# Prefix sums from a softplus in two parts, gates and loads further ahead, tokens turned before the scores, another join with the first MLP

## The chip, the cores and the metric

One core of one Trainium2 chip runs the whole program. The metric is the device time of one execution in microseconds (us). Five engines work at the same time, each through its own list of instructions in order: PE (matmuls and transposes, with weight loads that overlap them), DVE, ACT, POOL, and SP, which issues the DMAs here. Semaphores order them.

## What is computed

A gated linear attention over 4 batches, 8 heads, 768 tokens and a head size of 48, then two MLPs over the 384 channels:

```python
f = 1.0 / (1.0 + np.exp(-f_logit))
for t in range(S):
    state = f[:, :, t, :, None] * state + np.einsum('bhd,bhe->bhde', k[:, :, t], v[:, :, t])
    y[:, :, t] = np.einsum('bhd,bhde->bhe', q[:, :, t], state)
...
u = x + (xt @ U @ V)                    # tokens mixed, rank 32
x = u + np.maximum(u @ w_ch1, 0.0) @ w_ch2
h = np.maximum(x @ w_in, 0.0)           # second MLP, with a convolution of 3 taps
out = (h * sigmoid(conv(h))) @ w_out
```

Everything is float32. The second weights are float64 in memory and are put together from their two words on the chip.

## The kernel before

The attention works in 24 chunks of 128 tokens (6 for each batch), one pass of the loop `for i in range(1, NG)` for each, and chunk 0 ahead of it. For a chunk, `gate_max` and `gates` make sp = ln(1 + exp(-f)) (DVE or POOL, then two steps on ACT); `prefix` sums it along the tokens with one matmul with the triangular matrix `tri` (tile n), and ACT makes exp(-n) and exp(n) of it (a, b); `hats` multiplies q and k with these (qh, kh, from chunk 6 on POOL); `turn` transposes qh and kh (qTp, kTp) and ACT copies the result (qT, kT); `scores` multiplies them (s), `mask` applies the triangle on DVE (p, two instructions), `out_chunk` makes y from p and v and from qT and the state w, and adds to the state (kv); `state_end` brings the state on (wtmp on DVE, w on POOL), and `out_evac` copies y into u32 on ACT (u). Then `tokens` transposes a finished chunk's u (xt), ACT rounds it (xh), DVE makes the rest (xl), `mix_in` multiplies both with U (z), and after the sixth chunk of a batch `mix_z` (zu, zt, zz, zst) and six `mix_out` (mix, added into u on DVE) follow in the next three passes.

A value in two parts, such as xh and xl, is rounded to the type fp32r, and the remainder stands beside it; products of fp32r are made in one matmul each. `prefix` multiplies plain float32.

The order of the work on every engine is that of the code. In a pass i of the middle of the loop, f is loaded for chunk i + 4, k and q for i + 3, v for i + 2; `gate_max` and `gates` work on chunk i + 3, `prefix` and `hats` on i + 2, scores and output on i, `turn` on i + 1. All PSUM banks are named by hand: xt and the first `mix_out` of a pass share bank 0, n has bank 6. sp has two buffers, f, k and q three, v four.

DVE also prepares the first weights of the MLPs between this (cvt, cvg, `slot`, so many steps a pass as `slots(i)` says); the last step of such a piece runs at the head of the next pass (ACT cast, POOL difference w1l or w2l). One of them, cwp, transposes the taps on PE in bank 0.

After the last chunk, `mlps` runs the first MLP in units of 128 hidden columns (a, rh, rl, b), on halves of 512 tokens; `split1` makes uh and ul for a half. What is left of the attention is put between its matmuls by `hooks`.

Of the kernel before, what the change touches and what calls it, by code (L numbers as in the profile page):

```python
# [9 lines left out]
F32 = mybir.dt.float32  # L10
# [25 lines left out]
def kernel(  # L36
# [168 lines left out]
    def mlps(ms, banks, pieces, late, checks, hooks):  # L205
# [44 lines left out]
        def split1(t, i, engines):  # L250
            for kk in range(KD):
                split(u32[:, kk, t * T1 + i * HT:t * T1 + (i + 1) * HT], uh[:, kk, halves1[i]], ul[:, kk, halves1[i]], engines[i])

        def up1(u, i):
            t, j = divmod(u, J1)
            ps = bank(i, [128, HT], f"a{i}")
            up(w1hv, w1lv, j, halves1[i], (uh, ul), ps, lambda kk: hooks.pop((u, i, kk), int)())
            if (u, i) == (1, 0):
                down1(0, 0)
            rh = rg.tile([128, HT], F32R, tag="rh", name="rh")  # L260
            rl = rg.tile([128, HT], F32R, tag="rl", name="rl")
            nc.scalar.activation(out=rh, in_=ps, func=ACTF.Relu)  # L262
            nc.vector.scalar_tensor_tensor(  # L263
                out=rl, in0=ps, scalar=0.0, in1=rh.bitcast(F32), op0=ALU.max, op1=ALU.subtract)
            rt[1, u, i] = rh, rl
            hooks.pop((u, i, KD), int)()
            if j == J1 - 1:
                if t + 1 < NT:
                    split1(t + 1, i, (nc.vector, nc.gpsimd))
                else:  # L270
                    split_u(0, (i,))
# [157 lines left out]
        yield  # L429
        split1(0, 0, (nc.gpsimd, nc.vector))  # L430
        yield
        split1(0, 1, (nc.gpsimd, nc.vector))
        yield
# [58 lines left out]
        return banks.tile(shape, F32, tag=f"k{i}", name=name)  # L492

    tri = gc.tile([128, 128], F32, name="tri")
    ga = gc.tile([128, NG, NP], F32, name="ga")
    dr = gs.enter_context(tc.tile_pool(name="gdr", bufs=1, space=bass.MemoryType.DRAM))
    ends_d = dr.tile([NG, 1, NP * 128], F32, name="ends_d")
# [47 lines left out]
    def gates(g):  # L545
        sp = sps[g] = spt.pop(g)
        nc.scalar.activation(out=sp, in_=sp, func=ACTF.Exp, scale=-1.0)
        nc.scalar.activation(out=sp, in_=sp, func=ACTF.Ln, bias=one, scale=1.0)  # L548

    def prefix(g):  # L550
        n = bank(6, [128, DM], "n")
        mm(n, tri, sps.pop(g).rearrange("p h d -> p (h d)"), True, True)
        nv = n.rearrange("p (h d) -> p h d", h=H)
        b_ = ga1.tile([128, H, D], F32, tag="b", name="b")
        eng = nc.vector if g < DVE_HATS else nc.gpsimd
# [105 lines left out]
    def out_chunk(g):  # L661
        yt[g] = ps = bank(4, [128, KD, C], "y")
        qq, vv, pp = qT.pop(g), vt[g], pt.pop(g)
        started = set()

        def part(gr, lhsT, rhs):
            m, c = divmod(gr, 4)
            return c, ps[32 * c:32 * (c + 1), m, :], lhsT, rhs

        if g % NCH:  # L670
            w = w_t[g % 2]
            strips([part(3 * p + x, w[:, p, 32 * x:32 * (x + 1)], qq[:, p, :])
                    for p in range(NP) for x in range(3)], started)
        strips([part(3 * p + gr, vv[:, 128 * p + 32 * x:128 * p + 32 * (x + 1)], pp[j][:, p, :])
                for x, gr, j in ((0, 0, 0), (1, 1, 0), (2, 1, 1), (3, 2, 1)) for p in range(NP)], started)
        if (g + 1) % NCH:
            strips(state(g), set())
        vt.pop(g)

# [86 lines left out]
    with tc.manual_schedule():  # L766
# [5 lines left out]
        )  # L772
        nc.vector.memset(one, 1.0)
        nc.vector.memset(ga, 1.0)
        for t, x in ((a_t[0], 1.0), (q_t[0], 0.0), (k_t[0], 0.0)):
            nc.vector.memset(between(t), x)
        for t in w_t:
# [54 lines left out]
                    late_work.append(steps.pop(0))  # L832

        def slots(i):
            return (0, 6) if i == 1 else (0, 0) if i < 5 else (2, 2) if i < 8 else (1, 2)

        def mix_next():
            nonlocal mixed
# [26 lines left out]
        gates(3)  # L865
        ends(2)
        for i in range(1, NG):
            load_of(f"f{i + 4}")
            for x in "kq":
                load_of(f"{x}{i + 3}")  # L870
            load_of(f"v{i + 2}")
            if i < NG - 1:
                ends_back(i + 1)
            if i > 1 and i % NCH:
                state_end(i - 1)
            if EARLY_GATES <= i < NG - 3:
                gate_max(i + 3)
            follow = slot_end()
            n_mix = 2 if mixq else 0
            if i == FILL_FROM + 1:  # L880
# [1 line left out]
            hats = prefix(i + 2) if 1 < i < NG - 2 else None  # L882
            if i != CATCH_UP + 1:
                mix_next()
            scores(i)
            if i == CATCH_UP + 1:
                mix_next()
            if hats and i >= EARLY_GATES:
                hats()
            if zq:  # L890
# [5 lines left out]
            if zq:  # L896
                zq.pop()()
            if i < EARLY_GATES:
                gate_max(i + 3)
            if hats and i < EARLY_GATES:  # L900
                hats()
            lows = []
            if i > 1:
                lows.append(tokens(turned))
                turned += 1
            if i + 1 < NG:
                turn(i + 1, "qT")
            if zs:
# [2 lines left out]
                step()  # L911
            if zq:
                zq[0] = zq[0]()
            if i < NG - 3:
                gates(i + 3)
            if i < FILL_FROM:
                slot(slots(i)[1])
            if i == 1:
# [35 lines left out]
        tokens(NG - 1, 6)()  # L954
        next(mlp)
        last = {}

        def last_z():
# [6 lines left out]
            last["z"] = last["z"]()  # L965

        def last_casts():
            last["z"]()()

        def last_ends():  # L970
# [178 lines left out]
```

## Time and profile before

| What | Value |
| --- | --- |
| median of 3 runs | 654.68 us (654.08 to 655.6) |
| the profiled execution, its own time | 654.5 us |
| its span, first to last instruction | 652.8 us |
| PE busy | 641.3 us, 98% |
| DVE busy | 424.9 us, 65% |
| ACT busy | 275.2 us, 42% |
| POOL busy | 145.6 us, 22% |

Attention takes the first 149 us of the span, the first MLP goes on to about 441 us, the second fills the rest. A busy share says only that an instruction was under way; matmuls overlap, so what a step costs on PE is read from the chain of waits, where each piece stands with the time by which it moved the chain on. A row of the timeline gives start, duration, engine, line, operation, output and inputs, and in brackets how long the engine had been idle before and for whom it waited.

### The profile page before, as it was taken

The page shows a single profiled execution, that of the slowest core. Times are in us where ns is not written, and L with a number is a line of the kernel's source. Part 1 is how long each engine was busy: PE and PEld are TensorE (multiplying, and loading weights), DVE is VectorE, ACT ScalarE, POOL GpSimd, SP SyncE. Part 2 cuts the span into 40 slices and gives each one's busy share as a digit, 9 for nine tenths or more (in the row PEclk, how much of TensorE's full clock was granted, in tenths as well). Part 3 has the DMA queues.
Part 4 walks back from the last instruction along what each step waited for, and adds up shares of the span by engine and source line. Part 5 has one row for each costly group of instructions (what it writes and reads, how often), then busy time and mean ns, then how long its engine had stood idle before and what let it go on. Part 6 is the DMA issues. An engine that isn't in the chain of part 4 may idle for free.

```text
span 652.8 us, 12695 instructions
## 1 busy us (share of the span) xinstructions
PE 641.3 (98%) x5146; PEld 559.3 (86%) x5146; DVE 424.9 (65%) x663; ACT 275.2 (42%) x524; POOL 145.6 (22%) x181
## 2 busy tenths in 40 slices
PE   8999999999999999999999999999999999999995
PEld 6788778777888788888888888889999999999995
DVE  4868876566666665666665334226988777787762
ACT  5779677853223232222232111123544644634533
POOL 1176678441222222111112000001120110110000
PEclk9999999999999999999999999999999999999999
DMA  9988898810333330222220466100000200200202
GB/s 181 171 163 168 168 175 155 148 51 2 96 98 96 98 97 1 73 73 73 72 73 0 126 193 190 48 0 2 1 0 1 73 2 0 74 2 1 72 1 78
DMA packets 132661, 50.56 MB, mean 77 GB/s; under 512 B 112900, under 2 KB 128285, under 8 KB 132595
## 3 DMA queue, kind: packets, MB, share of 16 engines
q1 hardware_dynamic: 132594, 49.67, 31.2%
q8 instruction: 42, 0.69, 0.4%
q14 instruction: 25, 0.20, 0.1%
HBM read 44.89 MB, written 4.76 MB: 76 GB/s over the span
## 4 chain that ended last, share of the span: by engine, by line
PE 94%; DVE 2%; ACT 1%; issue 1%; DMA 0%; POOL 0%; POOLq 0%
PE a L76 38%; PE b L76 38%; PE y L76 5%; PE s L76 4%; PE n L76 2%; PE kTp L598 2%; PE xt L688 1%; PE qTp L598 1%; PE z L76 1%; PE mix L76 1%; PE kv L76 1%; DVE p L619 1%; DMA f<-in_f_logit_dram 0%; ACT sp L548 0%; PE row L76 0%
## 5 line engine op out<-in xcount | busy, mean ns | idle before, releaser
L262 ACT ACTIVATE rh<-a 128x512 fp32r<-128x512 f32 x72 | 43.1, 599 | 221.9 <-PE a L76 217.6
L263 DVE SCALAR_TENSOR_TENSOR rl<-a,rh 128x512 fp32r<-128x512 f32 x72 | 49.8, 692 | 109.1 <-ACT rh L262 109.0
L76 PE MATMUL a<-uh,w1l 128*128 128x512 f32 x216 | 84.4, 391 | 0.0
L76 PE MATMUL a<-uh,w1h 128*128 128x512 f32 x216 | 84.2, 390 | 0.0
L76 PE MATMUL a<-ul,w1h 128*128 128x512 f32 x216 | 84.1, 389 | 0.0
L76 PE MATMUL b<-rh,w2l 128*128 128x512 f32 x216 | 84.1, 389 | 0.0
L76 PE MATMUL b<-rh,w2h 128*128 128x512 f32 x216 | 84.0, 389 | 0.0
L76 PE MATMUL b<-rl,w2h 128*128 128x512 f32 x216 | 84.0, 389 | 0.0
L76 PE MATMUL b<-woh,w1h 128*128 128x384 f32 x264 | 70.4, 335 | 0.0
L318 ACT ACTIVATE c<-c 128x768 f32<-128x768 f32 x31 | 26.3, 847 | 62.4 <-DVE c L348 62.4
L76 PEld LDWEIGHTS a<-uh,w1l 128*128 128x128 f32 x216 | 40.5, 188 | 10.0 <-POOL w1l L79 1.8
L76 PE MATMUL a<-w2h,winh 128*128 128x384 f32 x192 | 49.0, 336 | 0.0
L76 PEld LDWEIGHTS b<-woh,w1h 128*128 128x128 f32 x264 | 48.0, 188 | 0.0
L76 PEld LDWEIGHTS b<-rh,w2h 128*128 128x128 f32 x216 | 40.6, 188 | 8.5
L76 PEld LDWEIGHTS b<-rh,w2l 128*128 128x128 f32 x216 | 40.5, 188 | 8.5
L76 PEld LDWEIGHTS b<-rl,w2h 128*128 128x128 f32 x216 | 40.5, 188 | 8.4
L76 PEld LDWEIGHTS a<-ul,w1h 128*128 128x128 f32 x216 | 40.6, 188 | 8.3
L76 PEld LDWEIGHTS a<-uh,w1h 128*128 128x128 f32 x216 | 40.6, 188 | 8.1
L79 POOL TENSOR_TENSOR ul<-u,uh 128x512 fp32r<-128x512 f32 (+1 forms) x15 | 19.1, 1295 | 127.0 <-ACT uh L105 127.0
L76 PE MATMUL b<-wol,w1h 128*128 128x384 f32 x132 | 44.3, 335 | 0.0
L304 ACT ACTIVATE h<-a 128x384 f32<-128x384 f32 x64 | 30.9, 496 | 29.3 <-PE a L76 26.0
L619 DVE TENSOR_TENSOR p<-s,tri 128x512 f32<-128x512 f32 x48 | 30.9, 686 | 17.9 <-PE s L76 17.6
(138 smaller groups left out, 1336.3 us busy)
## 6 DMA issues: line engine op xcount, KB each, us to landing
raw<-in_moe_w_ch_dram SPq DMA_DIRECT2D x48, 384.0 KB
f<-in_f_logit_dram SPq DMA_DIRECT2D x24, 192.0 KB
k<-in_k_dram SPq DMA_DIRECT2D x24, 192.0 KB
q<-in_q_dram SPq DMA_DIRECT2D x24, 192.0 KB
v<-in_v_dram SPq DMA_DIRECT2D x48, 96.0 KB
raw<-in_moe_w_in_dram SPq DMA_DIRECT2D x8, 384.0 KB
raw<-in_moe_w_out_dram SPq DMA_DIRECT2D x8, 384.0 KB
out_dram<-o SPq DMA_DIRECT2D x8, 192.0 KB
```

The lines of the kernel that those rows point to most:

```text
L76: nc.tensor.matmul(out=out, lhsT=lhsT, rhs=rhs, start=start, stop=stop, skip_group_check=True)
L79: eng.tensor_tensor(out=out, in0=a, in1=b, op=ALU.subtract)
L262: nc.scalar.activation(out=rh, in_=ps, func=ACTF.Relu)
L263: nc.vector.scalar_tensor_tensor(out=rl, in0=ps, scalar=0.0, in1=rh.bitcast(F32), op0=ALU.max, op1=ALU.subtract)
L304: nc.scalar.activation(out=h[:, 1 + hf.start:1 + hf.stop], in_=ps, func=ACTF.Relu)
L318: nc.scalar.activation(out=c, in_=c, func=ACTF.Sigmoid)
L598: nc.tensor.transpose(out=ps[:, p, :], in_=src[:, p, 0:MP], identity=ident)
L619: nc.vector.tensor_tensor(out=t, in0=sc[g][j], in1=tri.unsqueeze(1).to_broadcast([128, NP, C]), op=ALU.mult)
L688: nc.tensor.transpose(out=ps[:, m * 128:(m + 1) * 128], in_=u32[:, m, g * C:(g + 1) * C], identity=ident)
```

## The change

- `gate_split` is new. For chunks 8 to 23, DVE copies sp into fp32r (sph) and subtracts (spl); `prefix` then makes two fp32r matmuls with `trir`, an fp32r copy of `tri`, in place of the one of float32. Both new tiles have one buffer. The split of chunk i + 3 stands in pass i behind `state_end` and ahead of `prefix` of chunk i + 2.
- From pass 4 on, `gate_max` and `gates` work on chunk i + 4 (pass 4 does two chunks); k, q and v are loaded one pass sooner, f two passes sooner.
- `tokens` stands ahead of `scores`, behind `mix_in`. In the first chunk of a batch, the kv matmuls stand ahead of those of y.
- From pass 8 on, `slots` gives two steps of weights a pass and not three.
- The last xt stands behind the first three matmuls of the first MLP, and so does `split1` of the second half; the smallest gate (gp) is taken earlier.

```diff
+    def gate_split(g):
+        sp = sps.pop(g)
+        h_, l_ = [ga1.tile([128, DM], F32R, tag=t, name=t) for t in ("sph", "spl")]
+        src = sp.rearrange("p h d -> p (h d)")
+        nc.vector.tensor_copy(out=h_, in_=src)
+        sub(nc.vector, l_, src, h_.bitcast(F32))
+        sph[g] = h_, l_
...
-        mm(n, tri, sps.pop(g).rearrange("p h d -> p (h d)"), True, True)
+        if g in sph:
+            h_, l_ = sph.pop(g)
+            mm(n, trir, h_, True, False)
+            mm(n, trir, l_, False, True)
+        else:
+            mm(n, tri, sps.pop(g).rearrange("p h d -> p (h d)"), True, True)
...
-            return (0, 6) if i == 1 else (0, 0) if i < 5 else (2, 2) if i < 8 else (1, 2)
+            return (0, 6) if i == 1 else (0, 0) if i < 5 else (2, 2) if i < 8 else (1, 1)
...
-            if EARLY_GATES <= i < NG - 3:
-                gate_max(i + 3)
+            ahead = [g for g, on in ((i + 3, i <= AHEAD), (i + 4, i >= AHEAD)) if on and g < NG]
+            if i >= EARLY_GATES:
+                for g in ahead:
+                    gate_max(g)
+            if SPLIT_GATES <= i + 3 < NG:
+                gate_split(i + 3)
...
+            if i > 1 and not late_tokens:
+                lows.append(tokens(turned, 0 if i < NG - 2 else 6))
+                turned += 1
             scores(i)
...
-            lows = []
-            if i > 1:
-                lows.append(tokens(turned))
-                turned += 1
...
-        hooks.update({(0, 0, KD): last_z, (0, 1, 1): last_add, (0, 1, KD - 1): last_casts, (1, 0, 0): last_ends, (1, 0, 1): last_mix})
+        hooks.update({(0, 0, 0): lambda: tokens(NG - 1, 6)(), (0, 0, KD): last_z, (0, 1, 1): last_add, (0, 1, KD - 1): last_casts, (1, 0, 1): last_mix})
```

On PE, between the transposes of kh in pass 6 and the output of pass 7, there stood before (eight matmuls of s, two tiles in turn):

```order
L598 MATMUL kTp<-ident,kh_125 112x128 x4
L76 MATMUL n<-sp,tri 128x384
L76 MATMUL z<-xh,uhl 64x384
L76 MATMUL z<-xl,uhl 64x384
L76 MATMUL s_1132<-qT,kT 128x128
L76 MATMUL s_1133<-qT,kT 128x128
...
L688 MATMUL xt<-ident,u_76 128x128 x3
L598 MATMUL qTp<-ident,qh_122 112x128 x4
L76 MATMUL y<-qT,w_113 32x128 x12
```

and now:

```order
L619 MATMUL kTp<-ident,kh_126 112x128 x4
L78 MATMUL n<-sph,trir 128x384
L78 MATMUL n<-spl,trir 128x384
L78 MATMUL z<-xh,uhl 64x384
L78 MATMUL z<-xl,uhl 64x384
L711 MATMUL xt<-ident,u_76 128x128 x3
L78 MATMUL s_1174<-qT,kT 128x128
L78 MATMUL s_1175<-qT,kT 128x128
...
L619 MATMUL qTp<-ident,qh_123 112x128 x4
L78 MATMUL y<-qT,w_114 32x128 x12
```

The one matmul of n became two, and xt moved from behind s to ahead of it, so that only qTp and the first part of y stand between s and the first use of p.

On DVE, from the masks of pass 6 to the first mask of pass 7 (cvt and cvg are steps of the weights, w the state), there stood before:

```order
L79 TENSOR_TENSOR xl<-xt,xh 128x384
L128 TENSOR_SCALAR cvt<-raw 96x384
L129 SCALAR_TENSOR_TENSOR cvt<-raw,cvt 96x384
L646 TENSOR_TENSOR w_114<-kv,ga 48x4x48 x2
L130 SCALAR_TENSOR_TENSOR cvt<-raw,cvt 96x384
L137 TENSOR_SCALAR cvg<-raw 96x384
L619 TENSOR_TENSOR p_1027<-s_1012,tri 128x512
```

and now:

```order
L81 TENSOR_TENSOR xl<-xt,xh 128x384
L130 TENSOR_SCALAR cvt<-raw 96x384
L131 SCALAR_TENSOR_TENSOR cvt<-raw,cvt 96x384
L667 TENSOR_TENSOR w_115<-kv,ga 48x4x48 x2
L562 CAST sph<-sp 128x384
L81 TENSOR_TENSOR spl<-sp,sph 128x384
L132 SCALAR_TENSOR_TENSOR cvt<-raw,cvt 96x384
L139 TENSOR_SCALAR cvg<-raw 96x384
L640 TENSOR_TENSOR p_1064<-s_1049,tri 128x512
```

The two instructions of the split stand between the state and the mask, in front of the steps of the weights that were there.

On PE at the join, from the last output y, there stood before:

```order
L76 MATMUL y<-p_2871,v_129 32x128 x8
L76 MATMUL z<-xh,uhl 64x384
L76 MATMUL z<-xl,uhl 64x384
L688 MATMUL xt<-ident,u_76 128x128 x3
L76 MATMUL a_2927<-uh,w1h 128x512
```

and now:

```order
L78 MATMUL y<-p_2960,v_130 32x128 x8
L78 MATMUL z<-xh,uhl 64x384
L78 MATMUL z<-xl,uhl 64x384
L78 MATMUL a_2995<-uh,w1h 128x512
L78 MATMUL a_2995<-ul,w1h 128x512
L78 MATMUL a_2995<-uh,w1l 128x512
L711 MATMUL xt<-ident,u_76 128x128 x3
```

Three matmuls of the MLP came in between the output and the transposes that read it.

## Rows read from the trace of the kernel before

**Rows 1.** Chain of waits, pass 13: start us, us, what, number of instructions.

```profile
85.06 1.09 PE s L76 x16
86.15 0.48 PE xt L688 x3
86.62 0.44 PE qTp L598 x4
87.06 1.67 PE y L76 x56
88.73 0.34 PE kv L76 x32
89.07 0.58 PE kTp L598 x4
89.65 0.65 PE n L76 x2
90.30 0.35 PE z L76 x2
```

**Rows 2.** Chain of waits, second MLP: fp32r matmuls of 384 columns, new weights each.

```profile
457.97 3.12 PE b L76 x18
```

**Rows 3.** Chain of waits, places where it leaves PE or PE waited.

```profile
59.60 0.62 ACT sp L548
...
72.88 0.24 PE cwp L746
...
92.73 0.52 POOL w L644
...
129.38 1.41 DVE zst L79
...
148.03 0.49 ACT u L683
```

**Rows 4.** Groups by line and shape on DVE: busy us, mean ns of one | idle before.

```profile
L565 DVE TENSOR_TENSOR kh<-k,b 128x384 f32<-128x384 f32 x6 | 3.4, 558 | 0.2
L643 DVE TENSOR_TENSOR wtmp<-kv,w 48x192 f32<-48x192 f32 x32 | 11.2, 351 | 2.6 <-PE kv L76 2.1
L731 DVE TENSOR_TENSOR u<-mix,u 128x384 f32<-128x384 f32 x24 | 12.4, 547 | 8.6 <-PE mix L76 8.4
```

**Rows 5.** Timeline, POOL and DVE around 39 us, DVE at 48: start, us, engine, line.

```profile
38.69 1.10 POOL L644 TENSOR_TENSOR w<-wtmp,ga 48x192 f32<-48x192 f32 x2 [1.05 <-DVE wtmp L643]
39.03 0.39 DVE L128 TENSOR_SCALAR cvt<-raw 96x384 int32<-96x384 int32 x1
39.45 0.75 DVE L129 SCALAR_TENSOR_TENSOR cvt<-raw,cvt 96x384 int32<-96x384 int32 x1
...
48.11 1.25 DVE L129 SCALAR_TENSOR_TENSOR cvt<-raw,cvt 96x384 int32<-96x384 int32 x1
```

**Rows 6.** Timeline of DVE: the masks of passes 6 to 11 and 14 to 16.

```profile
46.05 1.29 DVE L619 TENSOR_TENSOR p<-s,tri 128x512 f32<-128x512 f32 x2 [1.53 <-PE s L76]
...
51.07 1.29 DVE L619 TENSOR_TENSOR p<-s,tri 128x512 f32<-128x512 f32 x2 [0.17 <-PE s L76]
...
56.66 1.29 DVE L619 TENSOR_TENSOR p<-s,tri 128x512 f32<-128x512 f32 x2 [0.94 <-PE s L76]
...
62.64 1.29 DVE L619 TENSOR_TENSOR p<-s,tri 128x512 f32<-128x512 f32 x2 [0.22 <-PE s L76]
...
68.73 1.29 DVE L619 TENSOR_TENSOR p<-s,tri 128x512 f32<-128x512 f32 x2 [0.22 <-PE s L76]
...
75.44 1.29 DVE L619 TENSOR_TENSOR p<-s,tri 128x512 f32<-128x512 f32 x2 [1.49 <-PE s L76]
...
91.77 1.29 DVE L619 TENSOR_TENSOR p<-s,tri 128x512 f32<-128x512 f32 x2 [1.03 <-PE s L76]
...
98.06 1.29 DVE L619 TENSOR_TENSOR p<-s,tri 128x512 f32<-128x512 f32 x2
...
104.62 1.29 DVE L619 TENSOR_TENSOR p<-s,tri 128x512 f32<-128x512 f32 x2 [0.88 <-PE s L76]
```

More of the change, by code (lines that the diff above doesn't have):

```diff
@@ L18 @@
 N_EARLY = 4
+SPLIT_GATES = 8
 EARLY_GATES = 4
@@ L22 @@
 WARM_UP = (7, 5)
+AHEAD = 4
 FILL_FROM = 22
@@ L256, in up1, with hook @@
             ps = bank(i, [128, HT], f"a{i}")
-            up(w1hv, w1lv, j, halves1[i], (uh, ul), ps, lambda kk: hooks.pop((u, i, kk), int)())
+            def hook(kk):
+                hooks.pop((u, i, kk), int)()
+                if (u, i, kk) == (0, 0, 0):
+                    split1(0, 1, (nc.gpsimd, nc.vector))
+            up(w1hv, w1lv, j, halves1[i], (uh, ul), ps, hook)
             if (u, i) == (1, 0):
@@ L431, in mlps @@
         yield
-        split1(0, 1, (nc.gpsimd, nc.vector))
-        yield
         n1 = NT * J1
@@ L494 @@
     tri = gc.tile([128, 128], F32, name="tri")
+    trir = gc.tile([128, 128], F32R, name="trir")
     ga = gc.tile([128, NG, NP], F32, name="ga")
@@ L548, in gates @@
         nc.scalar.activation(out=sp, in_=sp, func=ACTF.Ln, bias=one, scale=1.0)
+    sph = {}
+    def gate_split(g):
[5 more added lines that the diff above has]
+        sph[g] = h_, l_
     def prefix(g):
         n = bank(6, [128, DM], "n")
-        mm(n, tri, sps.pop(g).rearrange("p h d -> p (h d)"), True, True)
+        if g in sph:
[4 more added lines that the diff above has]
+            mm(n, tri, sps.pop(g).rearrange("p h d -> p (h d)"), True, True)
         nv = n.rearrange("p (h d) -> p h d", h=H)
@@ L673, in out_chunk @@
                     for p in range(NP) for x in range(3)], started)
+        if g % NCH == 0:
+            strips(state(g), set())
         strips([part(3 * p + gr, vv[:, 128 * p + 32 * x:128 * p + 32 * (x + 1)], pp[j][:, p, :])
                 for x, gr, j in ((0, 0, 0), (1, 1, 0), (2, 1, 1), (3, 2, 1)) for p in range(NP)], started)
-        if (g + 1) % NCH:
+        if g % NCH and (g + 1) % NCH:
             strips(state(g), set())
@@ L774 @@
         nc.vector.memset(ga, 1.0)
+        nc.vector.tensor_copy(out=trir, in_=tri)
         for t, x in ((a_t[0], 1.0), (q_t[0], 0.0), (k_t[0], 0.0)):
@@ L867 @@
         for i in range(1, NG):
[L868 to L871, printed above, removed]
+            more = sum(i > x for x in (2, 4))
+            for g in sorted({i + 4 + sum(i > x + 1 for x in (2, 4)), i + 4 + more}):
+                load_of(f"f{g}")
+            for x in [f"k{i + 3}", f"q{i + 3}", f"v{i + 2}"] * (i <= AHEAD) + [f"k{i + 4}", f"q{i + 4}", f"v{i + 3}"] * (i >= AHEAD):
+                load_of(x)
             if i < NG - 1:
@@ L884 @@
                 mix_next()
+            lows = []
+            late_tokens = i == CATCH_UP + 1
+            if i > 1 and not late_tokens:
+                lows.append(tokens(turned, 0 if i < NG - 2 else 6))
+                turned += 1
             scores(i)
-            if i == CATCH_UP + 1:
+            if late_tokens:
                 mix_next()
+                lows.append(tokens(turned))
+                turned += 1
             if hats and i >= EARLY_GATES:
@@ L898 @@
             if i < EARLY_GATES:
-                gate_max(i + 3)
+                for g in ahead:
+                    gate_max(g)
             if hats and i < EARLY_GATES:
                 hats()
-            lows = []
-            if i > 1:
-                lows.append(tokens(turned))
-                turned += 1
             if i + 1 < NG:
@@ L913 @@
                 zq[0] = zq[0]()
-            if i < NG - 3:
-                gates(i + 3)
+            for g in ahead:
+                gates(g)
             if i < FILL_FROM:
@@ L953 @@
         mix_in(NG - 2)
-        tokens(NG - 1, 6)()
-        next(mlp)
         last = {}
@@ L967, in last_casts @@
         def last_casts():
+            last_ends()
             last["z"]()()
```

## The prediction

> **What bounds the kernel now.** I read the table of engines first, then the chain of waits, then DVE's timeline, since the change takes work from PE and gives work to DVE. PE is busy for 98% of the span, but that says little, as matmuls overlap. The chain says more: through the middle of the attention it is PE without a gap. Pass 13 is shown [rows 1]: s, xt, qTp, y, kv, kTp, n, z, each starting where the last ended, together 5.60 us. That is also the distance from one pass's masks to the next's in pass 7, 51.07 to 56.66, 5.59 [rows 6]. A chunk that opens a batch has a shorter y (pass 6, 5.02), and a pass with two mix takes 6.09 (pass 9) [rows 6]. So microseconds taken from PE in the attention count in full, as long as nobody makes PE wait instead. The MLPs behind it are PE alone and are not touched.
>
> The second thing to see is how near DVE is. In front of the masks of passes 7, 9 and 10 it had been idle for 0.17 to 0.22 us only [rows 6], so it was all but full in passes 6, 8 and 9. And DVE is in front of PE: y needs the mask p. The places where the chain leaves PE are few: for sp on ACT, a transpose cwp behind a late DVE, w on POOL, zst on DVE, the copy u on ACT [rows 3].
>
> **The prefix sum.** n costs 0.65 in the chain, and float32 shows as two instructions [rows 1]. In its place come two fp32r matmuls of 384 columns with a weight load each. The nearest row is b of the second MLP: 18 of these in 3.12, so 0.173 each and 0.35 for two [rows 2]; z, the same pair with half the weights, is 0.35 as well [rows 1]. So 0.65 - 0.35 = 0.30 each, and 16 chunks (8 to 23) give **-4.8**. The pair could be no dearer than 0.40, if weight loads show, which would be 0.8 less in all.
>
> **Waits of PE that go.** Pass 8 took 62.64 - 56.66 = 5.98 [rows 6] against 5.59 for the same list; there n waited for sp, which ACT finishes just ahead [rows 3]. With the gates one pass earlier that is gone: **-0.4**. Pass 14 took 6.29, 0.70 over [rows 6], because y waited for w [rows 3] on a POOL that was behind after a late load of q. Loads go out a pass sooner, but POOL has the same work, so between 0 and 0.7 comes back; I take **-0.5**. At the join, xt waited for the copy u, 0.49 [rows 3]; now three matmuls of the MLP run there, and uh and ul for them were made before: **-0.45**. A little may be lost again behind it, where the last mix needs zst, which ACT and DVE finish just about then. Pass 10 took 6.71 [rows 6]; beyond 6.09 for a pass with mix and 0.24 for cwp itself [rows 3], 0.4 was a wait for DVE. cwp now stands one pass on, behind one step of weights instead of two, so I take **-0.1**. Together -1.45.
>
> **xt ahead of s** costs PE nothing; it covers ACT's copy kT, which n covered. But it also stood behind s, where it gave DVE 0.48 more for the masks. Now qTp, 0.44, and the 12 of y's 28 steps that need no mask, about 0.6 of 1.67 (an estimate by their number), are the cover [rows 1], and the first mask takes 0.7, half of the pair's 1.29 and a little [rows 6]. So a mask may be late by 0.3, not 0.8, before PE waits.
>
> **The split on DVE.** 16 times a cast and a difference of 128x384, both between SBUF tiles. They stand in front of the masks, and the cast waits for the n before it (one buffer), so only z, xt and s, 1.92 us [rows 1], lie between its start and the masks' at best. Behind them wait a step of weights and the masks, and for those y on PE. Prices: no row has this cast on DVE. The nearest one-input row is 0.39 behind wtmp; the nearest two-input row there is 0.75, because POOL's w was still running, until 39.79 [rows 5]; alone, a two-input one is 0.56 [rows 4]. POOL's w comes just then in most passes, so I take 0.39 + 0.75 and gaps, **1.17**. The bounds are 0.39 + 0.56 = 0.95 and 0.39 + 1.25 = 1.64 [rows 4, 5], the last when a long POOL instruction has just begun. One step of weights fewer a pass takes 0.4 to 1.2 out of passes 8 to 14 and puts it into 15 to 17, in the sum no gain.
>
> What this does, pass by pass: DVE's own time is the distance of two masks less the idle time.
> - Pass 6: 5.02 - 0.17 + 1.17 = 6.02, where PE needs 5.02 - 0.30 = 4.72: 1.3 over. Pass 7: 5.59 - 0.94 + 1.17 = 5.82 against 5.29: 0.5. Pass 8: 5.98 - 0.22 + 1.17, less 0.24 for a step that moves on (an estimate by the shortest step), is 6.7 against 5.29: 1.4. Pass 9: 6.09 - 0.22 + 1.17 - 0.8 for a step that moves on (an estimate by the 1.25 of [rows 5] against a short step) is 6.2 against 5.79: 0.45 [rows 6]. That is 3.65. But those DVE times hold waits for POOL like the 0.7 in 1.25 [rows 4, 5]; a mask that is late finds POOL's kh finished, so some of it goes. I take half, **+1.8**.
> - Pass 5 has its two steps of weights around the split: **+0.4**.
> - Passes 10 and 16: behind the second mix come an u 0.55, two wtmp 0.7, the split 1.17, a step 0.4, together 2.8 [rows 4, 5], while PE has n, z, xt, s, 0.35 + 0.35 + 0.48 + 1.09 = 2.27 [rows 1]. That is 0.55 late, less the 0.3 allowed: **+0.3** each.
> - Pass 15 has zst, four steps' worth of weights and mix in one; before, it took 6.56 [rows 6], 0.5 over. I take a further **+0.5**; between 0 and 1.2.
> - Passes 19 and 20: the chain runs over zz, zst and xl on DVE [rows 3], with wtmp and masks between, and the split comes in between too. The two savings of n there, 0.6, are eaten: **+0.6**.
> - The other passes have room. Sum **+3.9**.
>
> **The sum.** -4.8 - 1.45 + 3.9 = -2.35. On the span: 652.8 - 2.35 = 650.45; the profiled execution's own time is 1.7 more than its span, which gives 652.15, and the median of the runs is 0.18 above that execution: **652.3**.
>
> **A rule against the change.** In the trace the difference that waited took 0.34 until POOL's w ended, and then only 0.41, less than the 0.56 that one takes alone [rows 4, 5]. The Trainium skill, "SBUF — State Buffer", section "SBUF: two separate sides", says that VectorE and GpSimd share a pair of ports under an exclusive lock, which whoever comes first holds for the whole instruction while the other is fully blocked. By that the wait and a whole instruction add up, and the eight full passes lose 1.1 more in all: 653.4 instead of 652.3; it is the rule behind rival 2. That POOL's w holds DVE up, the trace agrees; that nothing overlaps, it does not.
>
> **Rivals.**
> 1. *DVE takes the split in its stride.* For it: at 0.95 instead of 1.17 eight full passes win 1.8, and where POOL, with its loads in time, is done earlier, the steps of 1.25 fall to 0.56. Then the +3.9 shrinks to 1 or less: 649.2. Against it: 0.17 us of idle time in pass 6 is 0.17 us.
> 2. *The gain is eaten, because the waits stay whole.* Each difference waits its 0.34 and then takes its whole 0.56 [rows 4, 5], so the pair costs 1.31 and the eight full passes 1.1 more; and passes 6 to 9 cost all of 3.65. 3.65 + 0.4 + 0.6 + 0.5 + 0.6 + 1.1 = 6.85 against 6.25: 655.3, the time of before within what can be told. For it: DVE and POOL both have work all the time there. Against it: the 0.41 behind the wait [rows 5].
> 3. *Slower: the split sets the pass.* If a long POOL instruction has begun whenever the difference comes, each pair costs 1.64, which is 0.47 more in the eleven passes that have no room, 5.2 on top of the forecast's 3.9: 657.5. It decides from a price of about 1.4 on, where the sum is nil. For it: the row of 1.25, and qh, which starts 0.5 after n, as does the difference. Against it: the difference is queued first, and the one that came second behind w got in at once.
> 4. That PE doesn't save what it should: the pair at 0.40 is 0.8 less, inside the range.
>
> **How the numbers follow.** Forecast (650.5 to 653.4) 0.46; rival 1, 0.18; rival 2, 0.22; rival 3, 0.14. A change of under 0.2%, 1.3 us, can't be told from none here: faster means under 653.4, slower over 656.0. So faster 0.64, same 0.22, slower 0.14. The range leaves out the far part of rivals 1 and 3: 649.0 to 656.3.
>
> **What would show it.** n in the chain at 0.35 for two, 16 times, confirms the first term. The split on DVE should show about 0.39 and 0.56 to 0.75. The masks' distance should be about 4.7 in passes 12 and 18, 5.3 in 13, and 5.5 to 6 in 6 and 7, with y waiting for p there; if passes 6 to 9 are no longer than before, rival 1 holds, and if passes 13 and 14 are longer too, rival 3. I am wrong altogether if the chain leaves PE for a load (f, k and q go out earlier and push one another), or for ACT in pass 4, which does two chunks' gates.

## The result, and the profile after

The changed kernel takes 662.3 us (median of 6 runs) where the kernel before took 655.1 beside it: a ratio of 1.0105, with a 95% interval of 1.0084 to 1.0126. It is slower by about 6.9 us, and the forecast was 2.4 us faster. The profiled execution took 662.64 us with a span of 660.9.

The table of engines of the kernel after: busy us, share of the span, instructions.

```profile
PE 642.4 (97%) x5146; PEld 560.8 (85%) x5146; DVE 440.2 (67%) x696; ACT 272.9 (41%) x524; POOL 148.2 (22%) x181
```

The shares of the engines alone don't show the loss. The chain of waits does. In a plain pass it reads as forecast (after; start us, us, what), to be set against [rows 1]:

```profile
93.41 0.58 PE qTp L619 x4
...
96.60 0.36 PE n L78 x2
96.96 0.35 PE z L78 x2
97.30 0.33 PE xt L711 x3
97.63 1.09 PE s L78 x16
```

n is 0.36 and not 0.65, and the list, with y, kv and kTp between, is 5.31 us long from the start of qTp to the end of s, 0.29 less than the 5.60 of before. But the masks of chunk 14 don't come 5.3 us after those of chunk 13, and elsewhere the chain leaves PE. The distances of the first masks of successive chunks show where the time went. All kernels of the table are described below; "6 to 7" is what the prediction calls pass 6.

| masks, us | before | after | no split | loads old | xt, join only | extra bytes |
|---|---|---|---|---|---|---|
| 4 to 5 | 5.59 | 6.53 | 5.59 | 6.14 | 5.59 | 5.59 |
| 5 to 6 | 5.25 | 4.72 | 5.24 | 4.96 | 5.24 | 5.25 |
| 6 to 7 | 5.02 | **9.24** | **9.47** | **8.02** | 5.02 | **9.68** |
| 7 to 8 | 5.59 | 6.64 | 6.76 | 6.58 | 5.58 | 5.36 |
| 8 to 9 | 5.98 | 6.13 | 5.59 | 6.20 | 5.98 | 6.17 |
| 9 to 10 | 6.09 | 6.58 | 6.19 | 6.58 | 6.47 | 6.06 |
| 10 to 11 | 6.71 | 6.37 | 6.00 | 6.36 | 6.00 | 6.00 |
| 11 to 12 | 5.71 | 6.40 | 6.13 | 6.38 | 6.13 | 6.12 |
| 12 to 13 | 5.03 | 4.96 | 5.03 | 4.96 | 5.01 | 5.01 |
| 13 to 14 | 5.59 | 5.58 | 5.58 | 5.59 | 5.59 | 5.59 |
| 14 to 15 | 6.29 | 5.38 | 5.59 | 5.39 | 5.85 | 5.87 |
| 15 to 16 | 6.56 | **7.67** | 6.39 | **7.67** | 6.07 | 6.27 |
| 16 to 17 | 5.99 | 6.36 | 6.00 | 6.36 | 6.00 | 6.00 |
| 17 to 18 | 5.71 | 5.88 | 5.70 | 5.88 | 5.71 | 5.71 |
| 18 to 19 | 5.03 | 4.71 | 5.02 | 4.71 | 5.02 | 5.02 |
| 19 to 20 | 6.71 | **7.56** | 6.37 | **7.56** | 6.37 | 6.38 |
| 20 to 21 | 6.55 | 5.78 | 6.45 | 5.79 | 6.94 | 6.93 |

Two losses can be seen. The first is one place, 6 to 7, with 7 to 8 behind it: 5.3 us more than before. There the chain runs over four engines, and in DVE's timeline (after; start us, us, line, [idle before, until what]) the masks stand behind a wait for a DMA:

```profile
49.42 1.26 DVE L131 SCALAR_TENSOR_TENSOR cvt<-raw,cvt 96x384 int32<-96x384 int32 x1
53.42 0.74 DVE L667 TENSOR_TENSOR w<-kv,ga 48x192 f32<-48x192 f32 x2 [2.73 <-DMA ga<-ends_d]
54.19 0.37 DVE L562 CAST sph<-sp 128x384 fp32r<-128x384 f32 x1
54.66 1.18 DVE L81 TENSOR_TENSOR spl<-sp,sph 128x384 fp32r<-128x384 f32 x1
...
56.61 1.29 DVE L640 TENSOR_TENSOR p<-s,tri 128x512 f32<-128x512 f32 x2
```

PE had little to do meanwhile, and its clock fell (after, by stretch: busy us of PE, PEld, DVE, ACT, POOL; granted clock, DMA share, GB/s):

```profile
40.00:50.00 10.00, 9.65 (x182) 7.53 (x181) 9.03 (x16) 6.59 (x15) 5.15 (x7) 1.00 0.92 181
50.00:60.00 10.00, 7.21 (x116) 5.52 (x115) 6.54 (x12) 5.49 (x12) 4.94 (x7) 0.72 0.78 157
60.00:70.00 10.00, 9.90 (x174) 8.39 (x174) 8.38 (x18) 8.76 (x19) 6.53 (x10) 0.94 0.95 189
```

The DMA that w waited for is the return of the row ends to ga. SyncE's queue shows why it was late. First the kernel after, then before (start us, us, what was issued):

```profile
43.03 0.50 SPq L605 DMA_DIRECT2D ga<-ends_d  x1
...
43.97 1.24 SPq L120 DMA_DIRECT2D raw<-in_moe_V_dram  x3
45.31 1.01 SPq L533 DMA_DIRECT2D f<-in_f_logit_dram  x2
46.41 0.59 SPq L533 DMA_DIRECT2D k<-in_k_dram  x1
47.05 1.27 SPq L533 DMA_DIRECT2D q<-in_q_dram  x1
48.41 2.61 SPq L529 DMA_DIRECT2D v<-in_v_dram  x2
51.08 0.50 SPq L605 DMA_DIRECT2D ga<-ends_d  x1
```

```profile
44.50 0.49 SPq L584 DMA_DIRECT2D ga<-ends_d  x1
```

The ga that w needs was issued at 51.08, before at 44.50: 6.58 us later. The masks of chunk 5 were only 1.85 us later than before (42.65 against 40.80), so the queue had fallen back by 4.7 us. The wait for ga is not alone there. The profile's chain comes to the second half of w (53.80) over ACT and over POOL's qh, which ended at 53.76, while the wait for ga had ended at 53.42. But w reads nothing of qh, so this link is the profile's inference; the experiments have to tell the causes apart.

The second loss is spread: DVE is full where the split stands. DVE's timeline ahead of the masks of chunk 10 (after) has no hole but one of 0.22 us:

```profile
69.38 1.29 DVE L640 TENSOR_TENSOR p<-s,tri 128x512 f32<-128x512 f32 x2
70.70 0.55 DVE L81 TENSOR_TENSOR zst<-zz,zst 32x384 fp32r<-32x384 f32 x1
71.27 0.56 DVE L81 TENSOR_TENSOR xl<-xt,xh 128x384 fp32r<-128x384 f32 x1
71.74 0.46 DVE L139 TENSOR_SCALAR cvg<-raw 24x128 int32<-24x128 int32 x1
72.42 1.17 DVE L754 TENSOR_TENSOR u<-mix,u 128x384 f32<-128x384 f32 x2 [0.22 <-PE mix L78]
73.51 0.73 DVE L664 TENSOR_TENSOR wtmp<-kv,w 48x192 f32<-48x192 f32 x2
74.27 0.37 DVE L562 CAST sph<-sp 128x384 fp32r<-128x384 f32 x1
74.75 0.68 DVE L81 TENSOR_TENSOR spl<-sp,sph 128x384 fp32r<-128x384 f32 x1
75.35 0.58 DVE L140 SCALAR_TENSOR_TENSOR cvg<-cvg,cvt 24x128 f32<-24x128 int32 x1
```

### The profile page after: what moved, and what is told of

Same layout as the page of the kernel before. It is cut to its first block, busy times and chain, and to the rows that moved or that the text cites. A ratio compares the mean times of both kernels' runs of the same rounds, so it can differ in the third digit from the quotient of the medians.

```text
span 660.9 us, 12738 instructions
## 1 busy us (share of the span) xinstructions
PE 642.4 (97%) x5146; PEld 560.8 (85%) x5146; DVE 440.2 (67%) x696; ACT 272.9 (41%) x524; POOL 148.2 (22%) x181
## 4 chain that ended last, share of the span: by engine, by line
PE 88%; DVE 6%; ACT 1%; DMA 1%; issue 1%; SPq 1%; POOL 0%; DVEq 0%; ACTq 0%
PE a L78 38%; PE b L78 37%; PE y L78 4%; PE s L78 2%; PE kTp L619 2%; DVE p L640 2%; PE n L78 1%; PE qTp L619 1%; DVE spl L81 1%; PE kv L78 1%; PE mix L78 1%; PE z L78 1%; SPq L533 1%; PE xt L711 1%; DMA f<-in_f_logit_dram 1%
## 5 line engine op out<-in xcount | busy, mean ns | idle before, releaser
L130 DVE TENSOR_SCALAR cvt<-raw 128x384 int32<-128x384 int32 (+3 forms) x44 | 37.9, 862 | 0.0
```

The costliest lines, as they stand in the source:

```text
L130: lambda: ve.tensor_scalar(out=t, in0=hi, scalar1=3, scalar2=0x3FFFFFFF, op0=ALU.logical_shift_left, op1=ALU.bitwise_and),
```

## The experiments

Sixteen kernels were run; each ratio is against the kernel before, run beside it. A profile is one execution, and executions differ (e7 has a median of 658.4, and its profiled execution took 661.8), so prices come from ratios and places from profiles. A difference of two ratios is turned into us with 656 us. The edits are shown shortened, with k(i+3) for the call that loads k of chunk i + 3.

| label | what differs | median us | ratio, interval |
|---|---|---|---|
| after | the change | 662.3 | 1.0105, 1.0084 to 1.0126 |
| e1_v_old | after, v at the old distance | 662.9 | 1.0104, 1.0085 to 1.0122 |
| e2_no_split | after, no split | 658.1 | 1.0028, 1.0010 to 1.0045 |
| e3_split_behind | after, split behind the masks | 669.8 | 1.0197, 1.0178 to 1.0217 |
| e4_v_old_split_behind | e1 and e3 | 669.0 | 1.0191, 1.0169 to 1.0213 |
| e5_loads_old | after, loads back (f one sooner) | 659.9 | 1.0037, 1.0017 to 1.0057 |
| e6_loads_old_split_behind_xl | e5, split behind xl | 660.2 | 1.0069, 1.0047 to 1.0091 |
| e7_before_soon_loads | before, loads a chunk sooner | 658.4 | 1.0027, 1.0011 to 1.0044 |
| e8_before_split_end | before, split at a pass's end | 665.5 | 1.0145, 1.0097 to 1.0193 |
| e9_join_xt_only | after, no split, loads and gates as before | 654.2 | 0.9973, 0.9958 to 0.9988 |
| e12_loads_old_no_split | e5, no split | 655.7 | 0.9995, 0.9978 to 1.0013 |
| e11_split_first_two_bufs | e5, split first, two buffers | 657.0 | 1.0016, 1.0002 to 1.0030 |
| e14_cast_on_act | e11, cast on ACT | 654.5 | 0.9987, 0.9970 to 1.0005 |
| g1_extra_bytes | e9 and five unused loads | 659.9 | 1.0071, 1.0052 to 1.0090 |
| f1_split_late_chunks | e14, chunks 14 to 23 only | 655.3 | 0.9994, 0.9977 to 1.0010 |
| f2_split_last_chunks | e14, chunks 19 to 23 only | 654.9 | 0.9994, 0.9982 to 1.0006 |
| j1_join_only | e9, xt at its old place | 654.7 | 0.9982, 0.9972 to 0.9993 |

### The queue, or the split?

The first theory (A) was that v, a pass sooner, waits for the buffer that y is still reading, and holds up the queue. The rival (B) was the split.

```diff
-[k(i+3), q(i+3), v(i+2)] * (i <= AHEAD) + [k(i+4), q(i+4), v(i+3)] * (i >= AHEAD)
+[k(i+3), q(i+3)] * (i <= AHEAD) + [k(i+4), q(i+4)] * (i >= AHEAD) + [v(i+2)]
```

> The changed kernel, with v's loads back at the old distance (v of chunk i+2 in pass i); f, k and q stay a chunk sooner. Theory A (the queue of loads): in the changed kernel v of chunk i+3 goes into the buffer that y of pass i-1 still reads, so SyncE stands in front of it for up to 2 us, and the row ends that come back to ga behind it are late; VectorE's w of chunk 6 then waits 2.7 us for ga, the split and the masks of pass 7 stand behind w, and that pass takes 9.24 us where it took 5.02 before. By A the wait for ga is gone here, pass 6 to 7 takes 5.5 to 6, the granted clock of 50 to 60 us is back over 0.9, and the time falls by 4 to 5.5 us, to 657 to 658.5. Theory B (the split's price): the split in front of the masks makes the loss and the wait for ga only fills a hole that is there anyway; then the time falls by less than 1 us.

No gain. The masks 6 to 7 took 10.89 us in its profile, and w still waited for ga, 4.7 us. So A in this form fell: it isn't v's buffer.

```diff
-SPLIT_GATES = 8
+SPLIT_GATES = 99
```

> The changed kernel without the split: all prefix sums are the one float32 matmul again (0.65 us each in the chain, 16 times 0.30 us more for TensorE), VectorE is rid of 16 casts and differences. Theory A (the queue of loads): the wait of w for ga stays, since loads and queue are the same, and so does most of the 9.24 us pass; -3.9 of the split in front of the masks and +4.8 for n nearly cancel: 661 to 664 us. Theory B (the split's price is what was mis-sized, some 9 us and more instead of 3.9): 657 us or less.

1.0028: 5.0 us less than after (0.0077 of 656), although every n now costs 0.30 more again. So the split costs 5.0 + 4.8 = 9.8 us in all, beside loads that all go out sooner. But 6 to 7 stayed at 9.47: the split isn't the reason for that place. Both theories were half right.

### Where the split should stand

```diff
-            if SPLIT_GATES <= i + 3 < NG:
-                gate_split(i + 3)
...
             mask(i, 0)
             mask(i, 1)
             if zq:
                 zq.pop()()
+            if SPLIT_GATES <= i + 3 < NG:
+                gate_split(i + 3)
```

> The changed kernel with the split moved behind the two masks of its pass on VectorE (the same cast and difference of the same chunk, used in the next pass). Theory A: the pass with the late w gets shorter by the split only (1 to 1.6 us), the other passes in which the split stands in the chain (5, 8, 9, 10, 15, 16, 17, 20) win 0.3 to 0.8 each, 2 to 4 us in all: 657.5 to 660 us; the wait of 2.7 us for ga stays. Theory B: the loss of 7 us goes whole, 653 to 655.5 us. A third way: behind the masks the difference meets GpSimd's instructions as often, and xl comes later for z: no change.

> Both edits: v's loads at the old distance and the split behind the masks. If the two losses are separate (theory A), the gains of the two runs add up: 6 to 9 us off the changed kernel, 653 to 656 us, and a plain pass such as 12 or 13 takes 0.3 us less than before. If both runs remove the same wait, the sum is no more than the larger of them.

Both are 6 us worse than after by the ratios, a miss on every theory. The chain of waits of e3 shows how (start us, us, what):

```profile
71.41 0.58 DVE sph L562
...
72.01 1.24 DVE spl L81
73.26 0.47 DVE xl L81
...
73.87 0.41 PE mix L78
...
75.39 0.64 PE z L78 x2
...
76.67 1.96 PE s L78 x16
```

The split made xl late, xl reads the bank that mix writes next, and PE waited some 2 us for it, three times (9 to 10, 15 to 16 and 20 to 21 are each 9.4 to 9.6 us). Then it ran at half its clock, as the stretches of 2 us show (e3; columns as above):

```profile
72.00:74.00 2.00, 0.13 (x1) 0.16 (x2) 1.84 (x3) 0.00 (x0) 0.84 (x1) 1.00 1.16 233
...
76.00:78.00 2.00, 2.00 (x16) 1.67 (x16) 0.44 (x2) 0.78 (x2) 1.84 (x4) 0.50 0.71 95
```

So xl is as near to the path as the masks.

```diff
             for step in lows + follow:
                 step()
+            if SPLIT_GATES <= i + 3 < NG:
+                gate_split(i + 3)
```

> The run before with the split moved behind xl and the step of weights on VectorE, where neither masks, xl nor the mix of that pass wait for it. In the run with the split right behind the masks, xl came late, and mix, which takes xt's bank, held TensorE for 2.1 to 2.3 us in passes 9, 15 and 20. If that was the whole reason why it was slower, the split now costs TensorE nothing in plain passes: 0.3 less in each than before, and about 3 to 5 us less than the run with the old loads, 652.5 to 656. If VectorE is simply full in passes 5 to 9 and 15 to 16, it moves the wait from the masks to n or u: within 1.5 us of the run with the old loads.

1.0069 against 1.0037 for the same loads with the split in the change's place, with intervals that overlap. There is no gain, where 3 to 5 us were hoped for: in the chain n now waits for the split (n stands behind spl 0.57 at 87.72), as the second half of the expectation had it. And in the kernel before, with no other edit:

```diff
             if i < FILL_FROM:
                 slot(slots(i)[1])
+            if SPLIT_GATES <= i + 3 < NG:
+                gate_split(i + 3)
```

> The kernel before with the split alone, at the end of a pass on VectorE (cast and difference of the chunk whose gates this pass made, ahead of the two u of a mix), loads, gates, xt and join as before. The pair of matmuls gives 16 x 0.30 = 4.8 us; a split costs 0.95 to 1.2 us of VectorE, which in passes 6 to 9 has 0.2 us idle in front of its masks. If the split can be hidden outside those: faster by 1.5 to 3 us, 653 to 655. If n has to wait for the split in each pass (in pass 13 the gates end at 88.76 and n comes at 89.95, which leaves 1.2 us): same or slower by up to 4 us.

Slower by 9.5 us, more than the worse of the two expectations. That one left 1.2 us between the gates and n; but n comes at 89.65 in the chain of before [rows 1], not at 89.95, and the 0.9 us that are left are less than a split. With gates three chunks on, the split waits for ACT, and n for the split; its list of waits from 35 to 135 us (engine, waiting for, us in total, times, longest):

```profile
PEld n L77 <- DVE sph L558: 5.7, 8, 2.0
PEld n L77 <- DVE spl L80: 5.1, 11, 0.9
DVE sph L558 <- ACT sp L550: 4.7, 6, 0.9
```

### The loads

```diff
-            more = sum(i > x for x in (2, 4))
-            for g in sorted({i + 4 + sum(i > x + 1 for x in (2, 4)), i + 4 + more}):
+            for g in sorted({i + 4 + (i > 3), i + 4 + (i > 2)}):
                 load_of(f"f{g}")
-            k(i+4), q(i+4), v(i+3)   from pass AHEAD on
+            k(i+3), q(i+3), v(i+2)
```

> The changed kernel with k, q and v loaded at the old distances and f only one chunk sooner than before (it has to be, for gates four chunks on), all else as changed: the split still stands ahead of the masks. Theory C (a debt of bytes): the DMA engines are 0.85 to 0.92 busy from the start to 120 us at 160 to 178 GB/s, so loads that go out sooner can't also land sooner; until pass 7 the changed kernel asks for f twice, k, q and v once more than before, 5 x 192 KB = 983 KB, 5.6 us at 175 GB/s, and f of chunk 10 and the row ends for w of chunk 6 come late by that. Here only one of the five is left: pass 6 to 7 falls from 9.24 us to 5 to 6.5, and the time falls by 3.5 to 5 us, to 657.5 to 659. Theory D: it is the order of ScalarE and VectorE (two chunks' gates in pass 4, two casts of vst and vh in front of a), which is unchanged: then pass 6 to 7 stays over 8.5 us and the time within 1.5 us.

1.0037: 4.5 us less than after, as theory C has it for the time. Its place is a miss: 6 to 7 still took 8.02 us in the profile, where 5 to 6.5 were expected, with one chunk of f left that is loaded sooner. The other way round, in the kernel before alone:

```diff
-            f(i+4), k(i+3), q(i+3), v(i+2)
+            k(i+4), q(i+4), v(i+3)   from pass 4 on
+            f(i+5)                   from pass 5 on
```

> The kernel before with one edit alone: f, k, q and v a chunk sooner from pass 4 on. Theory C: 4 x 192 KB more until pass 7, 786 KB, 4.5 us at 175 GB/s; pass 6 or 7 gets 3 to 4.5 us longer, and the later passes regain up to 2 us, since the waits for loads of q and f (4.5 and 4.0 us of GpSimd) go: slower by 2 to 4 us, 658 to 660.5. Theory D: no pass longer by over 1 us, faster by 0 to 1.5 us through those waits.

1.0027, slower by 1.8 us, just under what theory C expected. The mechanism is bare here, since there is no split and no other order (waits of e7, 44 to 58 us; then the piece of its chain):

```profile
POOL sp L543 <- DMA f<-in_f_logit_dram: 7.0, 1, 7.0
DVE w L647 <- DMA ga<-ends_d: 5.2, 1, 5.2
```

```profile
45.20 5.12 DMA f<-in_f_logit_dram
```

POOL waits 7.0 us for an f that takes 5.12 from issue to landing, and DVE 5.2 for ga. The next kernel moves no load that is used, to tell more traffic from the order of the loads and the buffers that they wait for:

```diff
+            for n, src in {3: [(0, f_logit)], 4: [(1, k), (2, q), (3, v)], 5: [(4, f_logit)]}.get(i, []):
+                extra(n, src, i + 6)      # 192 KB each, into tiles of their own
```

> The run with only xt and the join, and beside it five more loads of 192 KB into tiles that nothing reads: one in pass 3, three in pass 4, one in pass 5, that is as many bytes, and in the same queue, as the changed kernel asks for sooner; the loads that are used keep their distances. (The extra data is not used.) If the loss through the loads is a debt of bytes (983 KB at 175 GB/s are 5.6 us, of which the run with all loads sooner lost 2 to 4 in its time), passes 5 to 8 get 2 to 5 us longer, with VectorE waiting for ga or GpSimd for f, and the time is 2 to 4.5 us above the run with only xt and the join, 656.5 to 659. If it is not the bytes but which buffer a load waits for and what stands behind it in the queue, the extra loads, which wait for nothing, cost under 1 us.

1.0071 against 0.9973 without the extra loads (e9, below): 6.4 us, with both intervals about 1.2 us wide on each side, where 983 KB at 175 GB/s are 5.6 and 2 to 4.5 were expected. The place is the same one. g1's queue and its wait of w (44 to 58 us):

```profile
51.02 0.52 SPq L611 DMA_DIRECT2D ga<-ends_d  x1
```

```profile
DVE w L673 <- DMA ga<-ends_d: 4.2, 1, 4.2
```

ga at 51.02 where after had 51.08; it took 2.91 us to land. So five loads that nothing reads, in tiles of their own, are enough for a loss of this size, and no load that is used need be moved. They add bytes and also five more issues to SyncE's queue; these two were not told apart.

### One loss or two

```diff
-AHEAD = 4
-SPLIT_GATES = 8
+AHEAD = 99
+SPLIT_GATES = 99
...
+            load_of(f"f{i + 4}"), k(i+3), q(i+3), v(i+2) as before
```

> The changed kernel without the split and with all loads and gates at the old distances: what is left of the change is xt ahead of s and the join with the first MLP. If the losses of the split (5.0 us less without it) and of the sooner loads (4.4 us less with them back) are two and independent, both are gone here: 6.9 - 5.0 - 4.4 leaves 2 to 3 us faster than the kernel before, 653 to 655; the join alone was to give 0.45, so a part of that would be xt. If they are one loss seen twice (the split only hurts in a pipeline that the loads have emptied, or the other way round), 657 to 659.

0.9973: **faster than the kernel before by 1.8 us** (0.8 to 2.8), the lowest ratio of all kernels run. Adding up, 6.9 - 5.0 - 4.5 would be -2.6, so two losses that add up fit within the intervals, and one loss seen twice (657 to 659) does not. e9 keeps more than xt and the join: the two steps of weights a pass and kv ahead of y in a batch's first chunk are in it too, and none of these parts ran alone. In its one profile the b of the first MLP begins only 0.5 us sooner than before (156.59 against 157.08); where the rest of the 1.8 lies is not shown.

> The run with the old loads (f one chunk sooner, gates four chunks on), without the split. Against the run above it prices gates four chunks on with their f: 192 KB more until pass 7 is 1.1 us at 175 GB/s, so 0 to 1.5 us slower than the run above; against the run with the old loads it prices the split: 4 to 5 us less, 655 to 656.5, if that price is independent of the loads.

0.9995, 1.4 us over e9: gates four chunks on, with their 192 KB of f, cost about the 1.1 us of those bytes, with intervals that overlap. In its one profile 6 to 7 still takes 7.91 us, so that place is late even with one load sooner and no split. And 2.8 under e5, where 4 to 5 were expected and the split cost 5.0 with all loads sooner. So the split costs 2.8 to 5.0 net, and the loads 4.5 with the split and 2.2 without it (e2 against e12). Whether the two overlap by 2 us, or this is the intervals (about 1.2 us to each side of most ratios), stays open; that there are two is beyond them.

```diff
             lows = []
-            if i > 1 and not late_tokens: lows.append(tokens(turned, ...))   # ahead of scores
             scores(i)
...
+            if i > 1: lows.append(tokens(turned))                            # behind the masks
```

> The run with only xt and the join, with xt back behind the masks: the join (and the slots and the state of a batch's first chunk) alone. It tells how the gain of that run, 1.8 us against the kernel before, divides. The join was to give 0.45: then 655 to 655.5 here, and xt ahead of s has given 1.3 or so. If xt gives nothing, as qTp costs 0.14 more in the chain and xt 0.15 less: 654 to 654.5.

0.9982: most of the gain is without xt. What xt itself gives, 0.6 us, is inside the intervals. The gain left is 1.2 us (0.5 to 1.8), where the join was to give 0.45; whether the other parts give the rest was not run.

### DVE's time, or the split's place

```diff
-    ga1.tile(... "sph", "spl")      # one buffer
+    ga2.tile(... "sph", "spl")      # two
...
+            if SPLIT_GATES <= i + 3 < NG:
+                gate_split(i + 3)
             if i > 1 and i % NCH:
                 state_end(i - 1)
```

> The run with the old loads, the split standing first in its pass, ahead of w and wtmp of the state, with two buffers for its two tiles, so that it waits neither for n of its own pass nor for kv. VectorE has the same instructions as in the changed kernel. If the split's price is its place (in the changed kernel it starts only behind n and wtmp, 1.9 us ahead of the masks at best), passes 15, 16 and 20 lose 0.5 to 1 us each and plain passes 0.3: 1.5 to 4 us less than with the old loads, 655.5 to 658. If the price is VectorE's time itself (16 x 0.95 to 1.2 us in an engine that is full in passes 5 to 12), the place matters little: 658 to 660.

1.0016, 1.4 us under e5, at the lower end of what was expected from the place. Then the cast is taken off DVE:

```diff
         nc.scalar.activation(out=sp, in_=sp, func=ACTF.Ln, bias=one, scale=1.0)
+        nc.scalar.copy(out=hs[g], in_=sp)
...
-        nc.vector.tensor_copy(out=h_, in_=src)
```

> As the run above, with the cast on ScalarE, right behind the gates' logarithm (0.49 to 0.53 us of ScalarE for 0.36 of VectorE, 16 times); the difference stays on VectorE. If VectorE's time is the price, 16 x 0.36 = 5.8 us less of it gives 1 to 3 us against the run above. If ScalarE, 75% busy from 60 to 120 us, is as near to the path (kT, a and b stand behind the cast), no gain, or a loss of up to 3 us.

0.9987, another 1.9 us. By stretch (busy us of PE, PEld, DVE, ACT, POOL; granted clock, DMA share, GB/s), after first and then e14:

```profile
90.00:120.00 30.00, 28.30 (x571) 22.95 (x567) 27.51 (x50) 22.58 (x48) 22.07 (x30) 1.00 0.86 161
```

```profile
90.00:120.00 30.00, 28.83 (x555) 24.24 (x553) 23.72 (x44) 24.73 (x53) 25.10 (x33) 1.00 0.89 168
```

DVE falls from 27.51 of 30 us to 23.72, and ACT rises to 24.73. It is ACT that stands in e14's chain now:

```profile
83.93 0.62 ACT sp L554
...
84.58 0.35 ACT sph L557
...
85.00 0.47 ACT u L708
85.47 0.49 ACT kT L623
```

So the split's place (with its second buffers) and DVE's time each had a part, 1.4 and 1.9 us by the ratios, each with intervals that overlap; a kernel with the split then stands level with the one before, and no better.

```diff
-AHEAD = 4
-SPLIT_GATES = 8
+AHEAD = 10          # f2: 15
+SPLIT_GATES = 14    # f2: 19
```

> The run with the cast on ScalarE, but the split (and the gates four chunks on, and f a chunk sooner) begins late: only chunks 14 to 23 are split, f moves up in pass 9. If the split pays where TensorE bounds the pass and costs where VectorE does (passes 5 to 9), this keeps the 0.3 us of passes 12 to 14, 17 to 19 and 21 and loses in 15, 16 and 20 only: 1 to 2 us under the run with only xt and the join, 652 to 653. If the debt of 192 KB is paid in pass 9 or 10 as it was in pass 7, or ScalarE is the bound there: 654 to 656.

> The same with chunks 19 to 23 alone; f moves up in pass 14. Five pairs of matmuls can give 5 x 0.30 = 1.5 us; passes 17 to 19 lie in a stretch where VectorE and ScalarE are 58 to 60% busy and the DMA engines are 0.4 to 0.5 busy from 120 us on, so nothing should pay for it but pass 20: 0.5 to 1.2 us under the run with only xt and the join, 653 to 653.7; no gain if pass 20 takes it back.

Both 0.9994, a miss: neither beats e9. In f1 some plain passes gain (13 to 14 takes 5.05 against e9's 5.59, 16 to 17 5.72 against 6.00), but 12 to 13 takes 5.40 against 5.01, 10 to 11 7.18 against 6.00 and 15 to 16 7.29 against 6.07. In f2, 15 to 16 takes 7.28. In 10 to 11 of f1 and 15 to 16 of f2 the gates of two chunks are made. There the chain is on ACT, which runs the steps of sp twice, and mix waits for the copy u behind them (f2):

```profile
102.65 0.62 ACT sp L554
...
103.71 0.62 ACT sp L554
...
105.30 0.44 PE mix L78
```

From 15 to 21, f2's masks take 0.7 us more than e9's, so that one pass outweighs what the pairs give. But f1's 15 to 16 is as long without the second gates, so what these cost in f2 was not told apart from the split. The prediction feared just this of ACT, for pass 4, where it did not come: without a split, 4 to 5 is 5.59 before and in e2. f2's profile also has 6.90 us at 6 to 7, long before its edit begins and with the loads as before; the margin of the loads there is thin even so.

## Why the prediction was wrong, step by step

**The prefix sum, -4.8: right.** The pair stands whole in the chain twelve times, ten times at 0.35 to 0.37 and twice, behind a wait, at 0.49 and 0.55 (the single one of before took 0.84 and 0.91 in such places); rival 4 (0.40) is out.

**Waits that go, -1.45: right in size.** Pass 8's wait for sp is gone in e2 (8 to 9: 5.59 against 5.98, the 0.4 forecast). Pass 14 fell from 6.29 to 5.38, 0.3 of it n's, which leaves 0.6 for the wait for w, for 0.5 forecast; but e9, with the loads of before, has 5.85 there, so the sooner loads are not the whole reason. At the join the copy u no longer holds xt up:

```profile
155.60 0.49 PE z L78 x2
156.09 0.70 PE a L78 x3
156.79 0.33 PE xt L711 x3
```

From the last masks to the second product of the MLP, b, in the chain it is 11.28 us against 11.69: 0.41, for 0.45 forecast. Only the 0.1 of cwp did not come: it still stands in the chain behind DVE's u, at 85.79.

**The loads, 0: wrong, and worth 2.2 to 4.5 us** (1.8 alone, in e7; 6.4 as five unused loads, in g1). This is the step that failed altogether. The prediction said "Loads go out a pass sooner, but POOL has the same work", and took a load that is issued sooner for one that lands sooner. It never added up the bytes. They were there to be read: over stretches of 30 us the kernel before had a DMA share of 0.85 to 0.92 at 161 to 173 GB/s up to 120 us, so 983 KB asked for sooner pushed back what came behind, and behind stood the 1.8 KB of ga. "I am wrong altogether if the chain leaves PE for a load" is what happened: for f in e7 and for ga in e1, e2 and g1. In after, w waits 2.7 us for ga, though the chain as printed comes to w over ACT and POOL's qh.

**The split on DVE, +3.9: wrong in size; it is 7.6 to 9.8,** the net 2.8 to 5.0 and the 4.8 that n gives. The price of a pair was right: 1.16 us is its median here, 1.03 to 1.65 in all, for 1.17. What failed is the cover. "The other passes have room" and "I take half" let 16 pairs of 1.17 us come to 0.24 each on the path; measured it is 0.47 to 0.61. Against e2, and with n's 0.30 added, the split comes to 8.2 us in the two profiles from 4 to 21. The distances 4 to 6 cost 0.7 together, where 0.4 stood for pass 5; the passes 8 to 11 cost 0.57 to 0.84 each, 2.8 together; pass 15 costs 1.6, more than a whole pair, for 0.5; pass 19 costs 1.5, of which pass 20 gives 0.4 back, for 0.6 together; pass 16 0.66, for 0.3; and passes 12 and 13, which were said to be free, 0.23 and 0.30, about what n gave. The idle time in front of a mask [rows 6] was taken for room. But DVE's room lies between masks, in waits for kv and mix, and the split couldn't go there: its single buffer waits for n of the same pass, and it stood behind wtmp (74.27 in the timeline above). e11, with the split first and two buffers, has 1.4 us of it back.

**Rival 3** came nearest in time, for the wrong reason: it needed 1.64 a pair, which came once (1.65 at 54.19, beside POOL's kh).

**The rule against the change**, that of the Trainium skill, "SBUF — State Buffer", section "SBUF: two separate sides", is not borne out there either. POOL's kh had begun when spl came (after, timeline of POOL):

```profile
54.43 1.00 POOL L586 TENSOR_TENSOR kh<-k,b 128x384 f32<-128x384 f32 x1
```

spl, from 54.66 to 55.84, ended 0.41 after kh, where one alone takes 0.56; by the rule the whole 0.56 would come behind kh. It is the 0.41 of [rows 5] once more. Both rest on where the profile ends an instruction of POOL, which it gives roughly, so the 0.15 that is missing is a sign against the rule and not a proof.

**xt ahead of s: right, as nothing.** xt takes 0.33 and not 0.48, qTp 0.58 and not 0.44, and masks 1 to 3 lie 0.3 further apart in e9 than in j1; j1 and e9 are alike within their intervals.

With the measured sizes, the prices of the split and of the loads go in pairs, since each was measured with the other there or gone: -4.8 for n, -1.4 for the waits, 7.6 for the split and 4.5 for the loads give 5.9, and with 9.8 and 2.2 it is 5.8. The 1.4 of gates and f (e12 against e9) belongs to the loads too and makes it 7.2 to 7.3; the ratio says +6.9.

## What to carry to other kernels

Before loads are moved sooner, add up their bytes: where the DMA engines are as busy as here (0.85 to 0.92), a load that goes out sooner is a debt, and whatever stands behind it in the queue and is waited for pays it, here a row of 1.8 KB or the next f. Work that is moved to a busy engine costs a large part of its price in each pass in which that engine's queue from its last wait to the path's next need is full (0.57 to 0.84 of 1.16 us in passes 8 to 11, and more than the whole in 15); read that stretch of the timeline, not the engine's share or the idle time in front of one instruction. And undo a change of several parts one by one: here two parts lost more than the rest gave, and the rest alone was 0.27% faster than the kernel before.

## What the runs showed of the hardware

A wait of PE of some 2 us cost more than itself: in e3, PE was busy for 0.13 of 2 us, and 2 us later the granted clock was 0.50, the lower of its two levels (1.2 of 2.4 GHz): s took 1.96 us where it takes 1.09, z 0.64 for 0.35. In the kernel after, the stretch of 50 to 60 us had a mean of 0.72. A load of 192 KB took 5.12 us from issue to landing (f in e7, at a DMA share of 0.81 to 0.83), and the 1.8 KB of ga 2.2 to 3.0 (e5, e2, g1, e1), so size alone did not set the time of this small transfer. Whether the DMA engines or SyncE's queue hold it was not told apart: in the pass that waited, 50 to 60 us of the kernel after, the share was 0.78 and not 1. On DVE a cast of 128x384 into fp32r took 0.36 to 0.38 us and the difference 0.56 (at 45.97 in the kernel after, with POOL idle); on ACT the same cast took 0.51 (e14).
